# q and k arrive in 32x32 blocks and are turned by VectorE's stream transpose, from the third batch on

## The chip, the core and the metric

The kernel runs on one core of one Trainium2 chip. A core has five engines that work side by side, each with its own queue of instructions and joined by semaphores: TensorE (PE in the profile, with its weight loads as PEld), VectorE (DVE), ScalarE (ACT), GpSimd (POOL) and SyncE (SP), which here issues all DMAs. Data lie in HBM, in SBUF (on the core, 128 partitions) and in PSUM (eight banks into which TensorE writes). The metric is the device time of one execution in microseconds, the median of several runs; lower is better.

## The reference

The program is linear attention with an exponential feature map, followed by a mixer over tokens and channels. All inputs are float32 or float64 arrays; the shapes are batch 8, heads 8, sequence 576, head size 64, features 128.

```python
def phi(x):
    proj = einsum('bhsd,df->bhsf', x, w_phi)
    proj = proj - max(abs(proj), axis=-1, keepdims=True)
    return concatenate([exp(proj), exp(-proj)], axis=-1)
q_p, k_p = phi(q), phi(k)
kv  = einsum('bhsf,bhsd->bhfd', k_p, v)
z   = sum(k_p, axis=2)
num = einsum('bhsf,bhfd->bhsd', q_p, kv)
den = einsum('bhsf,bhf->bhs', q_p, z)[..., None] + 1e-06
x = (num / den) as (batch, seq, heads * 64)              # (8, 576, 512)
xt = x.transpose(0, 2, 1)
h = xt @ U @ V                                           # U (576, 32), V (32, 576): over tokens
u = x + h.transpose(0, 2, 1)
out = u + maximum(u @ w_ch1, 0) @ w_ch2                  # 512 -> 2048 -> 512
```

The order of the tokens matters to U, V and `out` alone: attention sums over tokens, and the channel part treats each token by itself.

## The kernel before

**Tiling.** Each batch has 576 tokens: 512 "main" ones, four tiles of 128 (NT = 4, SM = 512), and 64 "tail" ones (ST = 64). The tails of two batches share a tile, and all tails together form a ninth group of 512 tokens for the channel mixer. Heads are worked on in pairs: `Pair(b, j)`, 8 batches times 4 pairs. Main tokens are numbered `(p t)`: partition p of a tile holds tokens 4p to 4p+3, one in each of the four tiles, so that a partition's rows of q, k, v and `out` lie one after the other in HBM. Since `x` lies in that order, U is loaded as `(p t)` (line 155) and V's columns are permuted on VectorE (lines 176 to 179).

**Loading a pair.** `Pair.__init__` issues one DMA of 256 KB for k and one for q into `raw` (lines 248 to 251; two buffers, so k of one pair follows k of the pair before), then two for the tails into `t_r` (line 255, one buffer). `load_v` (line 262) issues four for v.

**Turning q and k.** A matmul contracts over partitions, so the 64 head dimensions of q and k must lie on partitions. `transposes` (line 276) does this on TensorE, with the identity `ident`: one for `t_r`, and for k and for q four 128x128 blocks into one PSUM bank `pT` (line 291), each block holding two tokens' 64 dimensions on its 128 partitions. In batches 0 and 1 (`split` false) one copy on ScalarE brings `pT` to SBUF as `T` (line 300), and projections run in full float32. From batch 2 on (`SPLIT = 2`) float32 is carried as a sum of two parts, high and low, of the faster type float32r: `stack` (line 271) writes the high part with a ScalarE copy (line 273) to 64 partitions and the low part with a VectorE subtraction (line 274) to the other 64, twice for each of k and q. One matmul over 128 partitions then multiplies both parts.

**The steps of a pair.** `s_project_k0`, `s_project_k1` (k features; line 371), `s_project_q0`, `s_kv0_q1` and `s_kv1` (q features and the sums over k and v; lines 394, 404, 411), `s_out0` and `s_out1` (lines 437, 450 and `normalize`). The features take the maximum of absolute values on VectorE for k, on GpSimd across partitions for q (line 335), and exponentials on ScalarE.

**The mixers.** `Tokens` multiplies by U and V (lines 521 and 537), writes u to HBM (line 539) for the later sum, and `Mixer` turns u (line 553) and runs 16 blocks of `hidden` (line 565, 12 matmuls of 128x512 into the one bank tagged `ph`, which line 570 on ScalarE and line 571 on VectorE empty into a high and a low part) and `add` (line 584, 12 matmuls). The weights come as float64 words and are converted on the core during batches 0 and 1 (`convert`, line 130, on ScalarE, VectorE and GpSimd).

**Order.** The main loop (line 775) works in a software pipeline over pairs: `cur` makes its outputs, `nxt` is projected, and `far`, two pairs ahead, is loaded and then turned in the middle of the step (`step(far.transposes)`, line 817, or in the list `fill`, line 795). The mixer of the batch before is cut into 32 chunks, which `Pace` spreads over the steps of the next batch, so that TensorE has long matmuls between the short ones of attention. The order that is written here is a priority: the framework plans each engine's instructions by a simulated timeline when the program is built, and sets semaphores; at run time each engine works through its queue in that order. Pools keep buffers by tag: `raw` two, `t_r`, `T0` and `T1` one each, PSUM three banks `at`, one `ph`, four `o`. The weights' loads are placed behind the last load of `far` (line 780).

Of the kernel before, what the change touches and what calls it, by code (L numbers as in the profile page):

```python
# [21 lines left out]
P = 128  # L22
# [3 lines left out]
def tile_kernel(  # L26
# [46 lines left out]
    def f32(ap):  # L73
        return ap.bitcast(F32)
# [76 lines left out]
    def load_uv():  # L151
# [3 lines left out]
            out=sv[:, 0:NT], in_=U[0:SM].rearrange("(p t) r w -> p t r w", t=NT))  # L155
# [13 lines left out]
        for cs in (slice(0, SM), slice(SM, S)):  # L169
# [6 lines left out]
            if cs.stop <= SM:  # L176
                ps_ = slice(cs.start // NT, cs.stop // NT)
                v_f = v_f.rearrange("r (p t) -> r t p", t=NT)
                vm = v_all[:, 0:SM].rearrange("r (t p) -> r t p", t=NT)[:, :, ps_]
# [55 lines left out]
    SPLIT = 2  # L235

    class Pair:


        def __init__(self, b, j):  # L240
# [5 lines left out]
            for n, src in enumerate((k, q)):  # L246
                m = raw.tile([P, 2, NT // 2, 2 * D], F32, tag="raw", bufs=2, name=f"raw{nm}_{n}")
                self.loaded = nc.sync.dma_start(
                    out=m.rearrange("p h s e -> p h (s e)"),
                    in_=src[b, hs, 0:SM, :].rearrange("h (p t) d -> p h (t d)", t=NT))  # L250
                self.raw.append(m)
# [10 lines left out]
        def load_v(self):  # L262
            self.vt, self.vb = (a[self.h0 // 2 % 2] for a in (vts, vbs))
            for g in range(2):
                nc.sync.dma_start(
                    out=self.vb[:, g, :, 0:D],
                    in_=v[self.b, self.h0 + g, 0:SM, :].rearrange("(p t) d -> p t d", t=NT))
# [8 lines left out]
        def transposes(self):  # L276
# [11 lines left out]
            for n in range(2):  # L288
                pT = self.ps(f"T{n}_", True)
                for c in range(NT):  # L290
                    nc.tensor.transpose(  # L291
                        out=pT[:, c * P:(c + 1) * P], in_=self.raw[n][:, c // 2, c % 2, :],
                        identity=ident)
                if self.split:
                    m = att.tile([P, 2, SM], F32R, tag=f"T{n}", name=f"T{n}_{nm}")
                    for s in range(2):
                        self.stack(pT[s * D:(s + 1) * D, :], m[:, s, :])
                else:
                    m = att.tile([P, SM], F32, tag=f"T{n}", name=f"T{n}_{nm}")
                    nc.scalar.copy(out=m, in_=pT)  # L300
# [62 lines left out]
        def project_k_split(self, g):  # L363
# [3 lines left out]
            for s in range(2):  # L367
# [5 lines left out]
                ts_ = slice(2 * s, 2 * s + 2)  # L373
# [71 lines left out]
        def out_main(self, s, qp, x):  # L445
# [7 lines left out]
            xo = x.rearrange("p (z s) c -> p s z c", s=2)[:, s, :, self.h0 * D:(self.h0 + 2) * D]  # L453
# [88 lines left out]
    class Mixer:  # L542
# [53 lines left out]
        def finish(self):  # L596
            g = self.g
            for t in range(4):
                if g < B:
# [3 lines left out]
                        out=out[g, 0:SM, :].rearrange("(p t) e -> p t e", t=NT)[:, t, :], in_=st)  # L603
# [257 lines left out]
```

## Time and profile before

| | |
|---|---|
| median of 3 runs | 1265.16 us (1265.14 to 1265.64) |
| span of the profiled execution (first to last instruction) | 1263.3 us |
| mean granted TensorE clock | 0.995 |
| first 193 us (batches 0 and 1, conversion of the weights) | TensorE busy 176.5 us |
| 193 to about 1065 us (batches 2 to 7, each about 139.7 us) | TensorE busy nearly throughout |
| from about 1068 us | the last mixers alone |
| q, k and v loads (lines 248, 255, 265, 268) | all on SyncE's queue |

The profile's page gives busy time of each engine, the granted clock and the DMA share over the span, and the chain of work that ended last. Other views of the same trace group instructions by line and shape (busy time, mean duration, idle time before them and what ended it), list waits by who waited for whom, give busy time in chosen stretches, or list instructions in order of time. An instruction's line is that of the kernel's file. "PE L291" is a matmul of line 291 on TensorE; "SPq" is a DMA issued by SyncE. The time of an execution as measured is 1.9 us longer than the profiled span.

### The profile page before, as it was taken

To read this page: it belongs to the slowest core of one execution; us is meant where nothing else is said; L and a number is where in the kernel's file an instruction comes from. 1 tells how busy PE (TensorE), PEld (TensorE's weight loads), DVE (VectorE), ACT (ScalarE), POOL (GpSimd) and SP (SyncE) were. 2 spreads that over 40 slices of the span, in tenths; PEclk is the share of its full clock that TensorE was granted. 3 is DMA by queue.
4 is the path that set the end of the run, shared out by engine and by line. 5 is a ranking of instruction groups with operands and counts; after the bars stand their busy time and mean duration, and the time that the engine had idled before them with its cause. 6 is when DMAs were issued, how large, how long until landed. Compare 5 with 4: busy or idle time off the path is not lost.

```text
span 1263.3 us, 17913 instructions
## 1 busy us (share of the span) xinstructions
PE 1234.8 (98%) x6941; PEld 1059.5 (84%) x6941; DVE 648.0 (51%) x1441; ACT 540.0 (43%) x1151; POOL 202.2 (16%) x154
## 2 busy tenths in 40 slices
PE   8989999999999999999999999999999999999997
PEld 7778777788888888888888888888888888788886
DVE  5877787745455545545455545654545542212111
ACT  6877776444443435344434434344534441111110
POOL 3444342111110111011111111111111110000000
PEclk9999998999999999999999999999999999999999
DMA  5695000411112002211122011211121002100001
GB/s 143 203 305 173 21 27 10 133 29 29 45 54 81 19 23 68 92 29 29 45 79 62 25 37 55 80 29 29 46 83 62 17 1 88 67 1 1 34 1 34
DMA packets 90100, 75.38 MB, mean 60 GB/s; under 512 B 51488, under 2 KB 76448, under 8 KB 89888
## 3 DMA queue, kind: packets, MB, share of 16 engines
q1 hardware_dynamic: 90016, 74.24, 19.2%
q8 instruction: 55, 0.90, 0.3%
q14 instruction: 29, 0.24, 0.1%
HBM read 55.35 MB, written 18.87 MB: 59 GB/s over the span
## 4 chain that ended last, share of the span: by engine, by line
PE 87%; ACT 5%; DVE 5%; issue 2%; DMA 1%; POOL 1%; SPq 0%; DVEq 0%; POOLq 0%; ACTq 0%
PE ph L565 30%; PE o L584 29%; PE kv_ps L411 7%; PE xp L450 7%; PE T L291 2%; PE pk L371 2%; PE pp L521 1%; PE xpt L437 1%; PE pt L553 1%; PE pq L394 1%; PE kv_ps L404 1%; ACT w_ab L138 1%; ACT w_ab L137 1%; PE pq L395 1%; ACT w_ab L140 1%
## 5 line engine op out<-in xcount | busy, mean ns | idle before, releaser
L565 PE MATMUL ph<-uT_hi,w 128*128 128x512 f32 x1152 | 388.2, 396 | 2.7 <-ACT uT_hi L231 2.3
L584 PE MATMUL o<-w,h_hi 128*128 128x512 f32 x1152 | 327.7, 396 | 2.2 <-ACT h_hi L570 2.0
L565 PEld LDWEIGHTS ph<-uT_hi,w 128*128 128x128 f32 x1152 | 215.9, 188 | 46.7 <-ACT uT_hi L231 3.2
L584 PEld LDWEIGHTS o<-w,h_hi 128*128 128x128 f32 x1152 | 211.4, 188 | 45.2 <-ACT h_hi L570 3.9
L571 DVE SCALAR_TENSOR_TENSOR h_lo<-ph,h_hi 128x512 fp32r<-128x512 f32 x144 | 99.2, 689 | 261.8 <-ACT h_hi L570 261.2
L565 PE MATMUL ph<-uT_lo,w 128*128 128x512 f32 x576 | 227.3, 395 | 0.5 <-DVE uT_lo L232 0.5
L570 ACT ACTIVATE h_hi<-ph 128x512 fp32r<-128x512 f32 x144 | 86.1, 598 | 306.2 <-PE ph L565 296.5
L584 PE MATMUL o<-w,h_lo 128*128 128x512 f32 x576 | 191.0, 396 | 0.0
L335 POOL PARTITION_ALL_REDUCE qp<-qp x64 | 126.5, 1979 | 340.4 <-ACT qp L334 331.3
L450 PEld LDWEIGHTS xp<-kv,qp 128*128 128x128 f32 x1024 | 122.7, 192 | 6.4 <-ACT qp L337 2.7
L565 PEld LDWEIGHTS ph<-uT_lo,w 128*128 128x128 f32 x576 | 108.7, 189 | 22.8 <-DVE uT_lo L232 1.7
L411 PEld LDWEIGHTS kv_ps<-vb,kp 128*128 128x128 f32 x1024 | 123.9, 195 | 4.2 <-issue 2.1
L450 PE MATMUL xp<-kv,qp 128*128 128x65 f32 x1024 | 123.3, 272 | 1.6 <-ACT qp L337 1.5
L584 PEld LDWEIGHTS o<-w,h_lo 128*128 128x128 f32 x576 | 106.6, 188 | 20.5
L411 PE MATMUL kv_ps<-vb,kp 128*128 128x65 f32 x1024 | 123.6, 275 | 0.0
L274 DVE TENSOR_TENSOR T<-T,T 64x512 fp32r<-64x512 f32 x96 | 66.1, 689 | 80.2 <-ACT T L273 78.9
L273 ACT CAST T<-T 64x512 fp32r<-64x512 f32 x96 | 55.9, 582 | 100.2 <-PE pq L395 73.5
L335 POOL PARTITION_ALL_REDUCE qp_t<-qp_t x32 | 25.3, 791 | 374.1 <-ACT qp_t L334 373.7
L325 ACT ACTIVATE kp<-kp 128x512 f32<-128x512 f32 x64 | 40.5, 632 | 63.0 <-DVE kp L322 48.7
L374 ACT COPY kp<-pk 128x256 f32<-128x256 f32 x96 | 35.4, 372 | 67.2 <-PE pk L371 67.0
L146 POOL INT64_ADD w_ab<-w_ab x32 | 44.4, 1387 | 88.1 <-DVE w_ab L142 49.6
L375 DVE TENSOR_TENSOR kp<-pk,kp 128x256 f32<-128x256 f32 x96 | 39.9, 418 | 30.3 <-ACT kp L374 30.0
(126 smaller groups left out, 1383.7 us busy)
## 6 DMA issues: line engine op xcount, KB each, us to landing
words<-in_moe_w_ch_dram SPq DMA_DIRECT2D x32, 512.0 KB, 7.6
raw<-in_k_dram SPq DMA_DIRECT2D x32, 256.0 KB, 2.9
raw<-in_q_dram SPq DMA_DIRECT2D x32, 256.0 KB, 3.0
vb<-in_v_dram SPq DMA_DIRECT2D x64, 128.0 KB, 2.6
u_dram<-x SPq DMA_DIRECT2D x32, 256.0 KB, 2.5
st<-u_dram SPq DMA_DIRECT2D x16, 512.0 KB, 4.3
out_dram<-st SPq DMA_DIRECT2D x32, 256.0 KB, 2.6
t_r<-in_k_dram SPq DMA_DIRECT2D x32, 32.0 KB, 2.2
```

What stands on the lines that cost most here:

```text
L146: nc.gpsimd.int64_add(a64, a64, b64)
L273: nc.scalar.copy(out=dst[0:D], in_=src)
L274: nc.vector.tensor_sub(dst[D:2 * D], src, f32(dst[0:D]))
L325: nc.scalar.activation(out=kp[:, :, 0:F], in_=kp[:, :, F:2 * F], func=AF.Exp)
L335: nc.gpsimd.partition_all_reduce(qp[:, 0, :], qp[:, 1, :], P, ReduceOp.absmax)
L375: nc.vector.tensor_tensor(out=k_w[:, ts_, :], in0=pk[:, :, 0, :], in1=kp[:, ts_, 0:F], op=ALU.add)
L411: nc.tensor.matmul(self.kv_v[:, f, g, :], kp[:, t, f * F:(f + 1) * F], self.vb[:, g, t, :], start=False, stop=(t == NT - 1), skip_group_ch ...
L450: nc.tensor.matmul(xv[:, c, :], qp[:, f, c * P:(c + 1) * P], self.kv[:, f, c // 2, :], start=(f == 0), stop=(f == 1))
L565: nc.tensor.matmul(ph, w1_part(f, l, c), r[:, c, :], start=(n == 0), stop=(n == 3 * NCC - 1))
L570: on_act = nc.scalar.activation(out=h_hi, in_=ph, func=AF.Relu)
L571: on_dve = nc.vector.scalar_tensor_tensor(out=h_lo, in0=ph, scalar=0.0, in1=f32(h_hi), op0=ALU.max, op1=ALU.subtract)
L584: nc.tensor.matmul(self.o[t], l[:, cs], w2_t[f][:, r, :], start=(f == 0 and n == 0), stop=(f == NFC - 1 and n == 2))
```

## The change

Three things change together.

1. **q and k of batches 2 to 7.** The pair's main tokens of k and of q are each loaded by eight DMAs of 32 KB instead of one of 256 KB. Each brings, for one head, one half of the 512 rows and one half of the 64 dimensions: 32 partitions, each with eight pieces of 32 float32 values (128 bytes), placed so that the tile consists of 32x32 blocks that only have to be turned in place. `nc.vector.transpose` turns all blocks of a 128x512 tile in one instruction, in SBUF. The eight TensorE transposes of the pair (four for k, four for q) and their PSUM banks are gone. The split in two parts (two ScalarE copies, two VectorE subtractions for each tensor) now reads SBUF.
2. **Token numbers.** Main tokens are numbered `(t p)`: tile t holds rows 128t to 128t+127. U is loaded so, V needs no permutation any more, `out` is written in 128 consecutive rows, and v of batches 2 to 7 is loaded as `(t p)`. The blocks of k's features (`ts_`) and of `x` (`xo`) move accordingly.
3. **Batches 0 and 1** keep their TensorE transposes. k and v stay in the old order there (only their sum over tokens counts), while q is loaded by four DMAs, each for one head and two of the four tiles, in pieces of 256 bytes.

```diff
-            out=sv[:, 0:NT], in_=U[0:SM].rearrange("(p t) r w -> p t r w", t=NT))
+            out=sv[:, 0:NT], in_=U[0:SM].rearrange("(t p) r w -> p t r w", t=NT))
...
-            if cs.stop <= SM:
-                ps_ = slice(cs.start // NT, cs.stop // NT)
-                v_f = v_f.rearrange("r (p t) -> r t p", t=NT)
-                vm = v_all[:, 0:SM].rearrange("r (t p) -> r t p", t=NT)[:, :, ps_]
...
-    SPLIT = 2
+    SPLIT, Q = 2, 32
...
-                m = raw.tile([P, 2, NT // 2, 2 * D], F32, tag="raw", bufs=2, name=f"raw{nm}_{n}")
-                self.loaded = nc.sync.dma_start(
-                    out=m.rearrange("p h s e -> p h (s e)"),
-                    in_=src[b, hs, 0:SM, :].rearrange("h (p t) d -> p h (t d)", t=NT))
+                m = raw.tile([P, 2, SM // 2], F32, tag="raw", bufs=2, name=f"raw{nm}_{n}")
+                if self.split:
+                    for i in range(4):
+                        rs = slice(i // 2 * (SM // 2), (i // 2 + 1) * (SM // 2))
+                        cs = slice(i % 2 * Q, (i % 2 + 1) * Q)
+                        for g in range(2):
+                            self.loaded = nc.sync.dma_start(
+                                out=m[i * Q:(i + 1) * Q, g, :].rearrange(
+                                    "c (j r) -> c j r", r=Q),
+                                in_=src[b, self.h0 + g, rs, cs].rearrange(
+                                    "(j c) r -> c j r", c=Q))
+                elif n == 0:
+                    self.loaded = nc.sync.dma_start(
+                        out=m, in_=src[b, hs, 0:SM, :].rearrange("h (p t) d -> p h (t d)", t=NT))
+                else:
+                    for g in range(2):
+                        for z in range(2):
+                            self.loaded = nc.sync.dma_start(
+                                out=m[:, g, z * P:(z + 1) * P].rearrange(
+                                    "p (s d) -> p s d", s=2),
+                                in_=src[b, self.h0 + g, 0:SM, :].rearrange(
+                                    "(s z p) d -> z p s d", s=2, z=2)[z])
...
+                order = "(t p) d -> p t d" if self.split else "(p t) d -> p t d"
...
-                    in_=v[self.b, self.h0 + g, 0:SM, :].rearrange("(p t) d -> p t d", t=NT))
+                    in_=v[self.b, self.h0 + g, 0:SM, :].rearrange(order, t=NT))
...
-                pT = self.ps(f"T{n}_", True)
-                for c in range(NT):
-                    nc.tensor.transpose(
-                        out=pT[:, c * P:(c + 1) * P], in_=self.raw[n][:, c // 2, c % 2, :],
-                        identity=ident)
                 if self.split:
                     m = att.tile([P, 2, SM], F32R, tag=f"T{n}", name=f"T{n}_{nm}")
+                    x_ = self.raw[n].rearrange("p h e -> p (h e)")
+                    nc.vector.transpose(out=x_, in_=x_)
                     for s in range(2):
-                        self.stack(pT[s * D:(s + 1) * D, :], m[:, s, :])
+                        here, there = (slice(i * D, (i + 1) * D) for i in (s, 1 - s))
+                        nc.scalar.copy(out=m[here, s, :], in_=x_[here])
+                        nc.vector.tensor_sub(m[there, s, :], x_[here], f32(m[here, s, :]))
                 else:
+                    pT = self.ps(f"T{n}_", True)
+                    for c in range(NT):
+                        nc.tensor.transpose(
+                            out=pT[:, c * P:(c + 1) * P],
+                            in_=self.raw[n][:, c // 2, c % 2 * P:(c % 2 + 1) * P],
+                            identity=ident)
...
-                ts_ = slice(2 * s, 2 * s + 2)
+                ts_ = slice(s, NT, 2)
...
-            xo = x.rearrange("p (z s) c -> p s z c", s=2)[:, s, :, self.h0 * D:(self.h0 + 2) * D]
+            xo = x.rearrange("p (s z) c -> p s z c", s=2)[:, s, :, self.h0 * D:(self.h0 + 2) * D]
...
-                        out=out[g, 0:SM, :].rearrange("(p t) e -> p t e", t=NT)[:, t, :], in_=st)
+                        out=out[g, t * P:(t + 1) * P, :], in_=st)
```

## The prediction

> **What bounds the kernel now.** I read the page first (engine shares), then busy time by stretches of the span, then TensorE's waits, then the timelines of TensorE, VectorE and SyncE through one batch. The page:
>
> ```profile
> PE 1234.8 (98%) x6941; PEld 1059.5 (84%) x6941; DVE 648.0 (51%) x1441; ACT 540.0 (43%) x1151; POOL 202.2 (16%) x154
> ```
>
> A busy TensorE (PE) can still be a PE that waits inside a share, so I look by stage. These are three stretches of the table by stretches: the first 64 us, the rest of batches 0 and 1, and one batch of the steady part (start:end, length, then busy us of each engine with its instruction count).
>
> ```profile
> 0.00:64.00 64.00, 57.80 (x381) 47.29 (x382) 46.60 (x123) 46.34 (x105) 27.18 (x38) 1.00 0.58 171
> 64.00:193.00 129.00, 118.72 (x680) 98.62 (x678) 101.95 (x204) 96.07 (x189) 54.31 (x39) 1.00 0.40 129
> 473.70:613.40 139.70, 139.03 (x816) 121.44 (x815) 74.33 (x171) 59.90 (x133) 18.64 (x12) 1.00 0.17 50
> ```
>
> In the steady batch PE is busy 139.03 of 139.70 us at granted clock 1.00, VectorE (DVE) 53%, ScalarE (ACT) 43%. In the first 193 us PE idles 6.2 + 10.3 = 16.5 us, while DVE and ACT are busy about three quarters of the time and the DMA engines 40 to 58%. So there are two stages with different limits: batches 0 and 1, where several things bind, and everything after, which is PE work end to end. All waits of the PE row from 334 to 1031 us (five batches; who waited, for whom, total, times, longest):
>
> ```profile
> PE ph L565 <- ACT uT_hi L231: 0.9, 2, 0.4
> PE ph L565 <- DVE uT_lo L232: 0.5, 2, 0.2
> ```
>
> 1.4 us in 697: there, a microsecond taken from PE is a microsecond off the end, as long as nothing new makes PE wait.
>
> **What the change removes: TensorE transposes.** From batch 2 on there are 6 x 4 = 24 head pairs, each with 8 transposes (4 of k, 4 of q). Matmuls overlap, so the price is not the duration of one but the distance between starts (start, us, operation, count):
>
> ```profile
> 544.58 1.03 PE L291 MATMUL T<-ident,raw 128*128 128x128 f32 x8
> 545.37 2.07 PE L584 MATMUL o<-w,h_hi 128*128 128x512 f32 x8
> 547.28 0.39 PE L565 MATMUL ph<-uT_hi,w 128*128 128x512 f32 x1
> 547.50 0.39 PE L565 MATMUL ph<-uT_lo,w 128*128 128x512 f32 x1
> ```
>
> Eight transposes take 545.37 - 544.58 = 0.79 us. The eight matmuls behind them take 1.91 us, where eight at the spacing of the undisturbed ones (547.50 - 547.28 = 0.22) take 1.76 to 1.82, the times being rounded to 0.01: the group costs another 0.09 to 0.15 us behind it. So a pair costs 0.79 (where small matmuls stand behind it anyway) to 0.94 us. I take 0.85: 24 x 0.85 = **20.4 us**, bounds 24 x 0.79 = 19.0 and 24 x 0.94 = 22.6.
>
> **What it adds on VectorE and ScalarE.** Two stream transposes of 128x512 a pair, which the trace does not show. The nearest rows are 128x512 operations from SBUF to SBUF (busy us, mean ns):
>
> ```profile
> L336 DVE TENSOR_TENSOR qp<-qp 128x512 f32<-128x512 f32 x64 | 47.5, 742 | 11.0 <-POOL qp L335 10.4
> L224 DVE TENSOR_TENSOR w<-w_ab,w 128x512 fp32r<-128x512 f32 x32 | 27.7, 877 | 3.6 <-ACT w L223 3.4
> L223 DVE CAST w<-w_ab 128x512 fp32r<-128x512 f32 x16 | 8.3, 519 | 3.4 <-POOL w_ab L146 3.4
> L180 DVE CAST v_all<-v_ab 128x512 fp32r<-128x512 f32 x1 | 1.1, 1120 | 0.0
> L182 DVE TENSOR_TENSOR v_all<-v_ab,v_all 32x512 fp32r<-32x512 f32 x1 | 1.1, 1096 | 0.0
> L274 DVE TENSOR_TENSOR T<-T,T 64x512 fp32r<-64x512 f32 x96 | 66.1, 689 | 80.2 <-ACT T L273 78.9
> ```
>
> Between 0.52 (a plain cast) and 1.12 us (a cast that reads with a stride); I take 0.74, the one in place over f32 (L336). The four subtractions a pair (L274) read SBUF alone instead of PSUM: 0.74 to 0.88 for 0.69, so at most +0.19 each. Together 2 x 0.74 + 4 x 0.19 = 2.2 us of DVE a pair, 9 a batch: 74 + 9 = 83 of some 136 us. That is far from a bound; it lies beside PE work and costs nothing itself. The ACT copies stay four a pair. What it can cost is place in the queue: DVE runs in order, and each of the two operations can stand in front of a split of `ph` (line 571), for which the one `ph` bank and so the next `hidden` wait. By the PE waits above, five batches lost 1.4 us to ACT and DVE; I allow 1 us for all six, bounds 0 and 3.
>
> **What it adds on SyncE and the DMA engines.** A split pair now issues 16 loads of 32 KB instead of 2 of 256 KB, in pieces of 128 bytes: 2 tensors x 2 heads x 512 rows x 2 halves = 4096 pieces. The costs of an issue (min/median/max ns of the issuing instruction), and landing times:
>
> ```profile
> L255 SPq DMA_DIRECT2D t_r<-in_k_dram x32: 615/627/747, 1.7 to 961.7; - x32
> ...
> raw<-in_k_dram SPq DMA_DIRECT2D x32, 256.0 KB, 2.9
> ...
> t_r<-in_k_dram SPq DMA_DIRECT2D x32, 32.0 KB, 2.2
> ```
>
> A t_r load has the new ones' 32 KB and an access of three dimensions, so I take its 0.62 us: 16 x 0.62 = 9.9 us of SP a pair, 5.0 for one tensor, and 2.2 to 2.9 to land: 12.8 us for both. Whether the engines keep up: in the window 509 to 515 us only two vb and two vt loads run, 1216 packets of 256 bytes; in 545 to 549 us nearly all is raw in packets of 1 KB.
>
> ```profile
> q1 hardware_dynamic: 1216, 0.30, 21.9%
> ...
> DMA packets 823, 0.60 MB, mean 149 GB/s; under 512 B 319, under 2 KB 822, under 8 KB 822
> q1 hardware_dynamic: 822, 0.58, 50.4%
> ```
>
> The first gives 0.219 x 16 x 6 us / 1216 = 17.3 ns a packet; the second, less 319 such, (32.3 - 5.5) us / 503 = 53 ns for 1 KB. A packet of 128 bytes should lie under 17.3 and cannot well exceed 53: 4096 / 16 = 256 on each engine, 4.4 us a pair, at most 13.6. I take 17.3; the SP queue is then the slower side. The Trainium skill ("DMA: Bandwidth & Descriptors", Rules for kernel authors) says against this change that transfers under 64 KB are mostly overhead, and (Anatomy of one DMA, for GpSimd's queue) fits about 2.0 us of fixed cost to each DMA; summed one behind the other, 16 of them would be an estimated 32 us a pair in place of the 12.8. The trace agrees with the fixed part (t_r lands in 2.2), and whether it is summed is the last rival.
>
> Is there room for 12.8 us? These are SP, DVE and PE rows around one pair:
>
> ```profile
> 545.22 0.55 SPq L248 DMA_DIRECT2D raw<-in_k_dram  x1
> 545.86 0.42 SPq L248 DMA_DIRECT2D raw<-in_q_dram  x1
> ...
> 547.46 0.69 DVE L274 TENSOR_TENSOR T<-T,T 64x512 fp32r<-64x512 f32 x1 [0.32 <-ACT T L273]
> 550.83 0.69 DVE L571 SCALAR_TENSOR_TENSOR h_lo<-ph,h_hi 128x512 fp32r<-128x512 f32 x1 [2.67 <-ACT h_hi L570]
> ...
> 556.00 0.69 DVE L274 TENSOR_TENSOR T<-T,T 64x512 fp32r<-64x512 f32 x1
> ...
> 559.98 0.40 PE L371 MATMUL pk<-w_hl,T 128*128 128x256 f32 x2
> ```
>
> Before, a raw buffer came free with PE's last transpose (545.37). Now it is held until the last split of the turned data: for k 548.2, for q 556.7 (q's second split waits until the previous pair's last use of T1 is over, as it does now). From 556.7, q's eight loads are issued by 561.7 and landed by 564.6. A batch of 139.7 us has four pairs, so the next transposes come some 35 us after 544.58, near 579.5, and the first projection from them another 15 later (for this pair 544.58 against 559.98). 15 us to spare; the other things behind the 14 added issues on SP (8.7 us: the pair's t_r and v loads, u_dram, st and out) have use times of the same order. So the loads cost nothing here, and would cost if a plan puts the turn close behind the landing (first rival).
>
> **Batches 0 and 1** keep their PE transposes, but q now comes in 4 loads of 256-byte pieces instead of 1, ahead of t_r, weights and v on the same queue.
>
> ```profile
> 2.54 0.61 SPq L255 DMA_DIRECT2D t_r<-in_q_dram  x1
> ...
> 4.94 0.45 PE L282 MATMUL tT<-ident,t_r 128*128 128x128 f32 x1 [0.98 <-DMA t_r<-in_q_dram]
> ```
>
> 4 x 0.62 less the one issue of 0.42 (545.86) is +2.1 us of SP in each of 8 pairs. The start hangs on this queue: PE's first real work waits for t_r, behind q. That moves by up to 2.1. Two more places can pay: pair 1, whose loads stand behind pair 0's, and a wait of the chain for v behind weights (start, us):
>
> ```profile
> 70.68 8.58 DMA vb<-in_v_dram
> ```
>
> Bounds 0 (the plan issues t_r first, later slack absorbs) and 6 (all three in full); I take 3.3. Against it, V's copy loses its stride: L180 and L182, 1120 and 1096 ns on DVE in a stretch where DVE is full, should fall towards L223's 519 and L224's 877, -0.8. Net **+2.5**. U's one load has four times as many pieces (512 of 256 bytes, 0.5 us on 16 engines at 17.3 ns); v in rows of 128, `kp` written in every second block and `out` in consecutive rows keep their counts and sizes; I cost all of these at nothing: they lie beside PE work.
>
> **Sum.** Profiled span 1263.3 us; the median of the runs is 1265.16, 1.9 more, which I carry over. 1263.3 - 20.4 + 1.0 + 2.5 = 1246.4 span, **1248** as measured. Own range: best 1265.2 - 22.6 - 0.8 = 1242; worst 1265.2 - 19.0 + 3 + 6 = 1255.
>
> **Rivals.**
> *DVE stands in front of a late load (slower).* The planner orders each engine's queue when the program is built, from its own timing. DVE is idle nearly half the time, so the plan may put a stream transpose right where it believes the load lands. If it believes raw's old landing of 2.9 us while the last piece comes 12.8 after the first issue, DVE stands still for 9.9 us, and the split of `ph` with it. The idle time ahead of h_lo (2.67 at 550.83) covers part; the rest, 7.2 us, reaches PE once a pair: 24 x 7.2 = 173, about 1421 us; with half the error 24 x 2.3 = 55, about 1303. It decides from (1265.2 - 1248) / 24 = 0.7 us of PE idle a pair. For it: the load's shape is new. Against: the plan has been close on DMA so far, as the only wait of a computing engine for a DMA from 334 to 1031 us is
>
> ```profile
> DVE xt L807 <- DMA u_dram<-xt: 0.9, 2, 0.4
> ```
>
> Chance 0.11 of slower; 0.05 that it takes part of the gain (1255 to 1262).
> *The gain is handed back.* DVE's two added operations a pair, 1.5 us, stand ahead of the split of `ph` at a moment without idle time in front, and half of that reaches PE: 24 x 0.75 = 18, so 1248 + 18 = 1266. Against: 0.3 us of waits a batch now. 0.05.
> *The loads serialise.* If 16 loads go one behind the other at t_r's 2.2 us, a pair's loads take 35.2 us; with 2 x 0.74 for the turn and 2.8 until the buffer is free (545.37 to 548.2), 39.5 a pair against 139.7 / 4 - 0.85 = 34.1: 24 x 5.4 = 130, about 1378 us. Against: two issues 0.64 us apart (545.22 and 545.86) overlap already, each landing in 2.9. 0.02.
>
> **How the numbers follow.** The forecast has 0.77. Its own range, 1242 to 1255, with the partial loss up to 1260 makes 8 in 10: 1242 to 1260. 0.2% is 2.5 us, about what a measurement here can tell. Faster by more: 0.77 + 0.05 = 0.82; within: 0.05; slower: 0.11 + 0.02 = 0.13.
>
> **What would show it.** L291 falls from 256 to 64 matmuls; a steady batch shrinks from 139.7 to about 136.4 us with PE still full; the DVE transposes read 0.5 to 1.1 us each; raw's loads take some 10 us of SP a pair and end over 10 us ahead of use; the first PE transposes of t_r start near 6 to 7 us instead of 4.94. I am wrong if DVE shows waits on raw of over 2 us in most pairs, if PE idles over 0.5 us a pair in steady batches, or if the first 193 us grow by more than 6.

## The result, and the profile after

The changed kernel takes 1259.2 us (median of 7 runs, 1253.6 to 1263.0) against 1265.6 us of before beside it (1265.1 to 1269.3): ratio 0.9933, 95% interval 0.9903 to 0.9962. That is about 8 us faster, where 17 were forecast: the right side and inside the range of 1242 to 1260, but less than half the size.

The page of the changed kernel, engine shares:

```profile
PE 1221.9 (97%) x6749; PEld 1044.6 (83%) x6749; DVE 680.5 (54%) x1489; ACT 541.6 (43%) x1151; POOL 204.0 (16%) x154
```

TensorE is busy 12.9 us less, but the span is only 7.1 us shorter (1256.2 against 1263.3). So TensorE is idle for longer: 34.3 us against 28.5. The table by stretches, for the first 64 us, the rest of batches 0 and 1, and one steady batch (from the first transposes of one mixer to those of the next), shows that "busy" is no fixed measure either; the third number from the right is the granted clock:

```profile
0.00:64.00 64.00, 56.17 (x343) 46.51 (x344) 39.51 (x107) 43.10 (x98) 25.39 (x36) 0.95 0.58 166
64.00:193.00 129.00, 119.79 (x702) 100.83 (x700) 101.79 (x213) 94.50 (x187) 53.49 (x39) 0.99 0.41 127
512.79:649.71 136.92, 136.37 (x783) 118.27 (x781) 79.25 (x178) 60.38 (x132) 18.73 (x12) 1.00 0.21 50
```

The steady batch went from 139.70 to 136.92 us with TensorE as full as before and 33 matmuls fewer in the record (32 transposes are gone). That is 2.8 us a batch, 0.70 us a pair. The first 64 us, however, hold 38 matmuls fewer than before, at a clock of 0.95.

What the turn became, groups by line (busy us, mean ns, then idle time just before and what ended it):

```profile
L311 DVE TENSOR_TENSOR T<-raw,T 64x512 fp32r<-64x512 f32 x96 | 70.8, 737 | 29.3 <-ACT T L310 27.0
...
L307 DVE STREAM_TRANSPOSE raw<-raw 128x512 f32<-128x512 f32 x48 | 34.1, 711 | 56.6 <-DMA raw<-in_q_dram 34.8 <-DMA raw<-in_k_dram 14.6 <-DMA t_r<-in_k_dram 2.5
L315 PE MATMUL T<-ident,raw 128*128 128x128 f32 x64 | 10.0, 291 | 0.0
```

A stream transpose of 128x512 takes 711 ns (0.74 was taken), a subtraction 737 (0.74 to 0.88). But VectorE stood 49.4 us in front of raw loads. Whether that costs anything is read one engine further on: the waits of the PE row from 334 to 1031 us, all of them:

```profile
PE pk L391 <- DVE uT_lo L228: 1.3, 5, 0.3
PE ph L585 <- ACT uT_hi L227: 0.3, 2, 0.2
```

1.6 us, as before (1.4). VectorE waits there in time that it has to spare.

**Three terms.** Each profiled span can be split into TensorE's idle time (span less busy), what the clock took (span times one less the mean granted clock), and the rest, TensorE's work at full clock. It is a rough split, since the clock has three digits (0.6 us), but it shows where the gain went. Before: 28.5 idle, 1263.3 x 0.005 = 6.3 to the clock, 1228.5 of work. After: 34.3 idle, 1256.2 x 0.009 = 11.3 to the clock, 1210.6 of work. The work fell by 17.9; idle time gave back 5.8 and the clock 5.0. These are single executions. The median run of the changed kernel had a clock of 0.988, so the typical run lost some 4 us more to it than the profiled one; so did the kernel before, whose median clock was 0.992 in 55 runs beside the experiments. Means over the runs stand further down.

**Where the idle time and the clock are lost.** The start of the changed kernel, SyncE and TensorE rows in order of time:

```profile
1.23 1.99 SPq L260 DMA_DIRECT2D raw<-in_q_dram  x4
3.26 0.74 SPq L269 DMA_DIRECT2D t_r<-in_k_dram  x1
4.05 0.61 SPq L269 DMA_DIRECT2D t_r<-in_q_dram  x1
...
6.26 0.45 PE L297 MATMUL tT<-ident,t_r 128*128 128x128 f32 x1 [2.30 <-DMA t_r<-in_q_dram]
```

q's four issues take 1.99 us (0.50 each), t_r is issued 1.5 us later and the first turn comes at 6.26 us in place of 4.94. The four issues stand in each pair of the first two batches, and the load of U, issued at 16.75 before, is issued at 22.11. From there a chain can be followed over ScalarE and VectorE to TensorE:

```profile
22.11 0.59 SPq L154 DMA_DIRECT2D u_st<-in_moe_U_dram  x1
...
25.74 0.38 ACT L137 ACTIVATE u_ab<-u_st 128x160 uint16<-128x160 uint16 x1 [1.29 <-DMA u_st<-in_moe_U_dram]
...
28.34 0.52 DVE L164 CAST u_all<-u_ab 128x128 fp32r<-128x128 f32 x3 [0.15 <-POOL u_ab L146]
...
31.52 0.42 DVE L449 TENSOR_TENSOR x<-xp,den 128x256 f32<-128x256 f32 x1
...
32.00 0.71 PE L424 MATMUL kv_ps<-vt,kp_t 128*128 128x130 f32 x4 [2.43 <-DVE x L449]
```

The same three places in the kernel before:

```profile
16.75 0.58 SPq L154 DMA_DIRECT2D u_st<-in_moe_U_dram  x1
...
20.95 0.39 ACT L137 ACTIVATE u_ab<-u_st 128x160 uint16<-128x160 uint16 x1 [1.06 <-DMA u_st<-in_moe_U_dram]
...
26.56 1.19 PE L291 MATMUL T<-ident,raw 128*128 128x128 f32 x8 [1.02 <-DVE x L429]
```

ScalarE waited for U before, too (1.06 us, now 1.29), but U's conversion now comes 4.8 us later in the run. It sits on VectorE just where the normalised outputs of a pair are wanted, and TensorE waits 2.43 us for those, where it waited 1.02. Then, in stretches of 2 us, the clock (third number from the right):

```profile
32.00:34.00 2.00, 2.00 (x18) 2.00 (x18) 1.31 (x3) 1.80 (x6) 1.07 (x1) 1.00 0.30 70
34.00:36.00 2.00, 2.00 (x13) 1.91 (x12) 0.19 (x1) 1.44 (x3) 0.48 (x1) 0.57 0.94 312
36.00:38.00 2.00, 2.00 (x11) 2.00 (x11) 1.97 (x6) 0.92 (x3) 1.66 (x2) 0.50 1.02 365
38.00:40.00 2.00, 2.00 (x9) 1.81 (x9) 0.90 (x2) 0.00 (x0) 1.00 (x2) 0.50 1.07 384
40.00:42.00 2.00, 2.00 (x6) 1.15 (x6) 0.72 (x2) 0.00 (x0) 0.00 (x0) 0.72 0.51 116
42.00:44.00 2.00, 2.00 (x20) 1.98 (x18) 1.85 (x6) 1.19 (x3) 0.86 (x1) 1.00 0.03 8
```

Two microseconds after the wait the clock halves, for some 6.8 us, while TensorE is completely busy: (0.43 + 0.50 + 0.50 + 0.28) x 2 = 3.4 us are lost. If the drop is put down to the wait, the 2.4 us have cost 5.8. Three other kernels with the same order of matmuls up to there show a wait of 2.45 us at the same place, and their clock falls there as well.

### The profile page after: what moved, and what is told of

Same layout as the page of the kernel before. It is cut to its first block, busy times and chain, and to the rows that moved or that the text cites. A ratio compares the mean times of both kernels' runs of the same rounds, so it can differ in the third digit from the quotient of the medians.

```text
span 1256.2 us, 18188 instructions
## 1 busy us (share of the span) xinstructions
PE 1221.9 (97%) x6749; PEld 1044.6 (83%) x6749; DVE 680.5 (54%) x1489; ACT 541.6 (43%) x1151; POOL 204.0 (16%) x154
## 4 chain that ended last, share of the span: by engine, by line
PE 84%; DVE 9%; ACT 4%; issue 1%; SPq 1%; DMA 1%; POOL 1%; DVEq 0%; ACTq 0%; POOLq 0%
PE ph L585 30%; PE o L604 28%; PE kv_ps L431 8%; PE xp L470 7%; PE pk L391 2%; PE pp L541 1%; DVE w L220 1%; PE kv_ps L424 1%; PE pq L414 1%; DVE uT_lo L228 1%; PE pt L573 1%; PE pq L415 1%; ACT w_ab L137 1%; ACT w_ab L138 1%; PE xpt L457 1%
## 5 line engine op out<-in xcount | busy, mean ns | idle before, releaser
L604 PE MATMUL o<-w,h_lo 128*128 128x512 f32 x576 | 198.0, 396 | 0.0
L311 DVE TENSOR_TENSOR T<-raw,T 64x512 fp32r<-64x512 f32 x96 | 70.8, 737 | 29.3 <-ACT T L310 27.0
L310 ACT CAST T<-raw 64x512 fp32r<-64x512 f32 x96 | 59.3, 618 | 29.2 <-PE pq L415 24.9
L357 ACT ACTIVATE qp<-qp 128x512 f32<-128x512 f32 x64 | 40.5, 632 | 66.2 <-DVE qp L356 65.8
L307 DVE STREAM_TRANSPOSE raw<-raw 128x512 f32<-128x512 f32 x48 | 34.1, 711 | 56.6 <-DMA raw<-in_q_dram 34.8
```

Source lines behind the costliest of these rows:

```text
L310: nc.scalar.copy(out=m[here, s, :], in_=x_[here])
L311: nc.vector.tensor_sub(m[there, s, :], x_[here], f32(m[here, s, :]))
L357: nc.scalar.activation(out=qp[:, 0, :], in_=qp[:, 1, :], func=AF.Exp)
L604: nc.tensor.matmul(self.o[t], l[:, cs], w2_t[f][:, r, :], start=(f == 0 and n == 0), stop=(f == NFC - 1 and n == 2))
```

## The experiments

Theory A: the forecast's main term holds, and what is missing was lost in batches 0 and 1, because q's four issues on SyncE delay everything queued behind them, and the idle time that this makes on TensorE then brings the clock down as well. Theory B: the turn on VectorE, or its small loads, is what gives the gain back. For each experiment the ratio to the kernel before that ran beside it is the measure, since that kernel's own median moved from 1265.6 to 1267.4 us between the sessions; the three terms are of the one profiled execution of each.

| kernel | median us | ratio to before (95%) | idle | to the clock | work |
|---|---|---|---|---|---|
| before | 1265.6 | 1 | 28.5 | 6.3 | 1228.5 |
| after | 1259.2 | 0.9933 (0.9903 to 0.9962) | 34.3 | 11.3 | 1210.6 |
| TensorE turns, rest of the change kept | 1275.9 | 1.0067 (1.0045 to 1.0089) | 32.7 | 14.0 | 1227.0 |
| one load of q | 1250.6 | 0.9869 (0.9846 to 0.9893) | 29.0 | 8.7 | 1210.7 |
| two loads of q | 1264.1 | 0.9969 (0.9951 to 0.9986) | 35.6 | 12.6 | 1210.6 |
| wide loads for the stream transpose | 1259.4 | 0.9945 (0.9923 to 0.9967) | 32.9 | 15.1 | 1209.1 |
| q's four loads from ScalarE | 1257.0 | 0.9916 (0.9902 to 0.9931) | 28.6 | 15.1 | 1211.4 |
| q's four loads behind t_r | 1252.4 | 0.9894 (0.9881 to 0.9907) | 30.1 | 11.3 | 1208.9 |
| q in four loads of long pieces | 1255.0 | 0.9910 (0.9897 to 0.9923) | 33.5 | 11.3 | 1210.3 |
| three filling matmuls for one | 1256.8 | 0.9925 (0.9913 to 0.9938) | 27.1 | 3.8 | 1223.5 |
| each turn done three times | 1263.5 | 0.9964 (0.9940 to 0.9987) | 36.4 | 19.0 | 1210.7 |
| behind t_r, two filling matmuls | 1258.1 | 0.9932 (0.9903 to 0.9961) | 30.4 | 12.6 | 1218.3 |
| from ScalarE, two filling matmuls | 1251.3 | 0.9871 (0.9836 to 0.9907) | 28.7 | 5.0 | 1216.2 |
| before, q's load behind t_r | 1265.5 | 0.9998 (0.9971 to 1.0025) | 27.5 | 8.8 | 1226.8 |

**TensorE turns again.** The loads in short pieces of batches 2 to 7 are replaced by q's four-load form for both tensors, and the transposes go back to TensorE; the numbering and the loads of batches 0 and 1 stay as changed.

```diff
...
-                elif n == 0:
+                if n == 0 and not self.split:
...
+                pT = self.ps(f"T{n}_", True)
+                for c in range(NT):
+                    nc.tensor.transpose(
+                        out=pT[:, c * P:(c + 1) * P],
+                        in_=self.raw[n][:, c // 2, c % 2 * P:(c % 2 + 1) * P],
+                        identity=ident)
...
-                    nc.vector.transpose(out=x_, in_=x_)
...
+                        self.stack(pT[s * D:(s + 1) * D, :], m[:, s, :])
...
```

> The new token numbers and the four loads of q, now for k too, in all batches, but every turn on TensorE as before the change. So only the stream transposes and their 128-byte loads are taken back. Theory A (the change takes 14 to 15 us of PE work away at full clock, and the early part, with q's loads and idle stretches that lower PE's clock, gives about 8 back): slower than the kernel before by 3 to 10 us, 1268 to 1275, with a mean clock below the 0.995 of before, and in the steady batches 139.7 us as before. Theory B (the loss is VectorE standing in front of late 128-byte loads, in all batches): like before, 1264 to 1267, since nothing waits for such loads here.

Measured 1275.9 us, ratio 1.0067, just above the range of Theory A. This splits the result in two. The turn alone, from this kernel to the changed one, is worth 1.0067 - 0.9933 = 1.34%, 17 us (12 to 22 by the two intervals); the rest of the change costs 0.67%, 8.5 us (5.7 to 11.3). The forecast had 20.4 - 1.0 = 19.4 and 2.5 for the two. Here the work is 1227.0, nearly as before: what is lost is all idle time and clock.

**One load of q.** q of batches 0 and 1 goes back to one load in the old order.

```diff
-                elif n == 0:
+                else:
                     self.loaded = nc.sync.dma_start(
                         out=m, in_=src[b, hs, 0:SM, :].rearrange("h (p t) d -> p h (t d)", t=NT))
-                else:
-                    for g in range(2):
-                        for z in range(2):
...
```

> The changed kernel, but in batches 0 and 1 q comes in one load of 256 KB as before the change, so that its tokens there stand in the old order, which this kernel does not put right; all else is the changed kernel. Theory A: the first turn starts near 4.9 us again, the clock drops between 30 and 100 us go, mean clock 0.993 or more, 1250 to 1254 us. Theory B: no change, 1257 to 1261.

1250.6 us, ratio 0.9869: 0.64% less than the changed kernel, 8.1 us (some 5 us to either side by the intervals). That is the whole price of the early part as far as can be measured. What is left, 1.31% or 16.6 us less than the kernel before, is what the turn alone gives, and so the numbering of U, V and `out` costs nothing that can be seen. Its early stretches, to be set beside those above:

```profile
0.00:64.00 64.00, 57.98 (x380) 47.52 (x381) 45.56 (x120) 46.25 (x105) 27.23 (x38) 1.00 0.64 191
64.00:193.00 129.00, 124.02 (x697) 104.92 (x697) 101.37 (x210) 95.15 (x188) 53.91 (x39) 0.96 0.38 118
```

380 matmuls in the first 64 us, as before (381), at full clock; the changed kernel had done 343. The drops of the clock up to 100 us did not all go, as Theory A had it: the stretch from 80 to 96 us reads 0.68.

**Two loads of q.**

```diff
                     for g in range(2):
-                        for z in range(2):
...
+                        self.loaded = nc.sync.dma_start(
+                            out=m[:, g, :].rearrange("p (t d) -> p t d", t=NT),
+                            in_=src[b, self.h0 + g, 0:SM, :].rearrange("(t p) d -> p t d", t=NT))
...
+            order = "p (s z) c -> p s z c" if self.split else "p (z s) c -> p s z c"
+            xo = x.rearrange(order, s=2)[:, s, :, self.h0 * D:(self.h0 + 2) * D]
```

> The changed kernel, but in batches 0 and 1 q comes in two loads, one per head, in the same 256-byte pieces, with the tiles of x numbered to match. Two issues less on SyncE in each of eight pairs. Theory A: between the changed kernel and the one with a single load, 1253 to 1258. Theory B: no change, 1257 to 1261.

1264.1 us: worse than four loads, a miss for Theory A in the form "so much per issue". The first turn starts at 5.78 us, between the two, but TensorE is idle for 35.6 us; 3.8 us of that lie between 48 and 64 us, and from 64 to 80 us the clock is 0.70. So the number of issues alone does not set the price; why this arrangement is the worst was not found.

**Wide loads.** The loads of 128-byte pieces are replaced by one load of 256 KB a tensor in every batch.

```diff
-                if self.split:
-                    for i in range(4):
...
-                elif n == 0:
+                if n == 0 or self.split:
                     self.loaded = nc.sync.dma_start(
```

> The changed kernel with the stream transposes, but from batch 2 on k and q come in one load of 256 KB each, in rows of 1 KB as before the change, so that the turned blocks do not hold what they should; the arithmetic is otherwise left as it is. Theory A: VectorE's waits for raw shrink, but PE is not held by them in the steady batches (0.6 us a batch), so at most 2 us are won outside clock drops: 1255 to 1260. Theory B: the waits of 57 us in front of the stream transposes fall below 15 and 6 us or more are won: 1248 to 1253.

1259.4 us, ratio 0.9945 against 0.9933, the intervals overlap. The change's most striking feature, 384 loads of 128-byte pieces in place of 48 large ones, is free here as far as can be measured, and a steady batch takes 136.9 to 137.0 us with either, but for one of 138.6 in the changed kernel in which the clock fell. VectorE's waits in front of raw did not shrink but grew (35.7 and 31.9 us for q and k, against 34.8 and 14.6): the plan puts the turn right behind the landing, whatever the load. Theory B falls for the loads.

**Where q's issues stand, and what they carry.** Three kernels tell issue time from piece size and place.

```diff
-                            self.loaded = nc.sync.dma_start(
+                            nc.scalar.dma_start(
```

> Theory A (the early price of some 8 us is SyncE's issue time: q's four loads stand in front of t_r, v, U and V, and what arrives late lets TensorE and then its clock fall): with q's four loads of batches 0 and 1 issued by ScalarE, SyncE has its old queue, U's load is issued near 16.8 us again, and the time falls to 1249 to 1254; ScalarE pays some 2 us a pair where it has slack. Theory B (the 256-byte pieces of q cost, whoever issues them): 1257 to 1261.

```diff
-                else:
-                    for g in range(2):
-                        for z in range(2):
-                            self.loaded = nc.sync.dma_start(
...
             self.t_r = raw.tile([P, 2 * D], F32, tag="t_r", bufs=1, name=f"t_r{nm}")
...
+            if not self.split:
+                m = self.raw[1]
+                for g in range(2):
+                    for z in range(2):
+                        self.loaded = nc.sync.dma_start(
...
```

> The same four loads of q on SyncE, issued behind t_r instead of in front of it. Theory A in its narrow form (the first turn of t_r, 1.3 us late, is what costs): back to 1250 to 1254. Theory A in its wide form (v, U and V behind the pairs' loads are late too, and they still are): 1255 to 1260, with the first turn near 4.9 us. Theory B: 1257 to 1261.

```diff
+                            ps_ = slice(z * D, (z + 1) * D)
+                            rs = slice(z * (SM // 2), (z + 1) * (SM // 2))
...
-                                out=m[:, g, z * P:(z + 1) * P].rearrange(
-                                    "p (s d) -> p s d", s=2),
-                                in_=src[b, self.h0 + g, 0:SM, :].rearrange(
-                                    "(s z p) d -> z p s d", s=2, z=2)[z])
+                                out=m[ps_, g, :],
+                                in_=src[b, self.h0 + g, rs, :].rearrange(
+                                    "(p t) d -> p (t d)", t=NT))
```

> q of batches 0 and 1 in four loads, but of 1024-byte pieces and in the old order of tokens (its rows come out in another order there, which this kernel doesn't put right). Theory A (number of issues): as the changed kernel, 1257 to 1261. Theory B (size of the pieces, or the order of the tokens): as with one load, 1249 to 1253.

Four loads of long pieces leave TensorE as idle as four of short ones (33.5 against 34.3, and 29.0 with one load), and their first turn is as late (6.74 us). So the size of the pieces is not the cause of the idle time. Its time, 1255.0, lies between the two expectations; the profiled execution is within 1.1 us of the changed kernel's (1255.1 against 1256.2, both at a clock of 0.991), and the intervals of the two ratios overlap. Issued behind t_r the first turn starts at 4.51, idle time falls to 30.1, and the time to 1252.4 (ratio 0.9894), although U is still issued at 22.27 us: the place of t_r is the larger part, so the narrow form of Theory A. Issued by ScalarE they leave TensorE as idle as before the change (28.6), with the first turn at 5.26 and U issued at 20.36; yet 1257.0 came out, a time of Theory B's range and not of Theory A's. The clock takes 15.1 us: against the kernel with one load (29.0 and 8.7) it is the whole difference. So the idle time goes with the issues on SyncE, and the clock's loss here does not.

**The clock itself.** `keep_busy` runs filling matmuls on zeros at steps that have no mixer work; it does three in place of one here.

```diff
-                    keep_busy(1, True)
+                    keep_busy(3, True)
...
-                keep_busy(1, True)
+                keep_busy(3, True)
```

> The changed kernel with three filling matmuls in place of one at each step where the mixer has nothing to give. If the early price is paid through TensorE's clock, which falls after stretches with idle time, the clock stays up and the time falls to 1250 to 1256 at a mean clock of 0.993 or more. If the price is the idle time itself, the filling changes nothing or adds up to 10 us: 1259 to 1270.

Between the two expectations, and the table says why. The clock now reads 1.00 where it had fallen (start of the stretch, TensorE busy, clock; the changed kernel had 13.52 and 1.00, then 16.00 at 0.79):

```profile
16.00:32.00 16.00, 15.87 (x108) 12.52 (x107) 10.57 (x37) 9.90 (x23) 4.40 (x6) 1.00 0.48 123
32.00:48.00 16.00, 15.65 (x111) 13.03 (x111) 12.64 (x32) 10.49 (x27) 6.84 (x7) 1.00 0.59 177
```

Against the changed kernel the clock gives back 7.5 us and idle time 7.2, and the filling, 62 more matmuls, is 12.9 us of work: 1.8 us remain. So most of the early drops do follow TensorE's gaps, since filling the gaps takes them away (the mean clock is 0.994 to 0.998 in five runs), but the filling costs almost what it gains.

**VectorE's dose.** Each turn is done three times in place.

```diff
-                    nc.vector.transpose(out=x_, in_=x_)
+                    for _ in range(3):
+                        nc.vector.transpose(out=x_, in_=x_)
```

> Each stream transpose is done three times in place (three turns give what one gives), so VectorE gets another 4 x 0.71 us a pair. The question is why a pair gave 0.70 us and not 0.85. Theory S (the transposes' own spacing and their neighbours on TensorE; VectorE's work lies beside it): the time stays within 4 us of the changed kernel, a steady batch stays at 136.9 to 137.3 us. Theory D (VectorE's queue hands back 0.15 us a pair for its 1.42 us of turning): another 0.30 us a pair, 24 x 0.30 = 7 us at least, and a steady batch of 138.1 us or more.

68 us more of VectorE (101.7 for 34.1) cost 0.31%, 4 us. Four steady batches of the profiled execution, the slowest of twelve:

```profile
382.74:519.65 136.91, 136.29 (x783) 118.23 (x781) 89.40 (x194) 61.32 (x132) 19.39 (x12) 1.00 0.22 51
519.65:656.86 137.21, 136.57 (x782) 118.33 (x781) 89.91 (x194) 60.99 (x132) 19.38 (x12) 1.00 0.22 51
656.86:797.14 140.28, 138.19 (x783) 119.52 (x781) 89.62 (x193) 61.24 (x132) 19.03 (x12) 0.99 0.21 49
797.14:934.97 137.83, 136.57 (x783) 118.25 (x781) 90.54 (x195) 61.13 (x132) 19.04 (x12) 1.00 0.22 51
```

Two of them are as short as with one turn; in the other two TensorE waits for an operation of VectorE on x (2.2 us in all), and the clock reads 0.99 in one of them. Theory S holds for the single turn: VectorE hands back nothing that can be seen in the steady part. With three times the dose the edge is near: two of the four batches lie above its 137.3.

**Two combinations.** Each of the two better orders with two filling matmuls in place of one (the edits are those above).

> q's four loads behind t_r, and two filling matmuls in place of one at the early steps. If the loss left in that order is mostly the clock (0.990 against 0.997 with three filling ones), and a second filling matmul costs about half of what two cost: the clock reads 0.994 to 0.997 and the time 1247 to 1252. If the filling costs as much as the clock gives back, as with three: 1252 to 1257.

> q's four loads from ScalarE's queue, and two filling matmuls in place of one. At full clock this order is worth as much as one load of q (span times clock 1239.6 against 1240.1); if the clock is all that it lacks: 1248 to 1252 at 0.994 or more. If filling costs what it gives: 1255 to 1258.

The first is a miss: 1258.1, worse than without filling (1252.4). The clock is not the reason: over all runs of the two kernels the clock takes 8.9 us with the filling and 12.2 without, but idle time and work together are 9.1 us more, where the same filling costs 5.4 in the other order. Why it costs more here was not found. The second does what it was meant to: 1251.3 us, ratio 0.9871, 0.62% less than the changed kernel, with the new numbering in full. It loses 5.0 us to the clock and 28.7 to idle time, about as the kernel before (6.3 and 28.5), and pays 4.8 us of work for the filling. It beats both kernels.

**A control.** In the kernel before, q's one load of batches 0 and 1 is issued behind t_r.

> The kernel before, with one thing moved: in batches 0 and 1 q's one load is issued behind t_r and not in front of it. No count or size changes. Theory A (SyncE's issue time is the price): the first turn starts 0.5 us earlier, and the time is that of before or less, 1262 to 1267. Theory C (any edit of the first batches gives another plan for them, and plans differ by several microseconds through idle time and clock): more than 3 us away from before, to either side, with a mean clock that differs by 0.003 or more.

1265.5 us, ratio 0.9998: nothing, although the first turn starts at 4.34 in place of 4.94. So not every edit of the first batches moves the time, and Theory C, as a general rule, falls. It also says that a 0.6 us earlier first turn is worth nothing by itself in the old plan.

## Why the prediction was right and wrong

**What bounds it** was right: a steady batch is TensorE end to end before and after, and TensorE's waits there stayed at 1.6 us.

**The transposes** were taken at 0.85 us a pair, with bounds of 0.79 and 0.94. Measured: 0.70 in the steady batch (2.8 / 4), (1227.0 - 1210.6) / 24 = 0.68 by the work of the kernel with TensorE's turns, 17 / 24 = 0.71 by its time (of these 17 us some 4 are a difference in the clock, by the table below). The mechanism was right; by the steady batch the term is 16.8 us in place of 20.4, and by every measure below the lower bound of 19.0. The eight starts do go (0.77 us a pair over four batches), but the cost added for the group behind them did not come back, and the transpose of t_r, which used to run into them, now has 0.07 us before the next start in place of 0.03 (16 of them over four batches: 1.08 us for 0.45).

**VectorE and ScalarE** were right in price (711 ns for 740) and in being beside the path: the allowed 1 us was not needed, and three times the dose cost 4 us. **The first rival** is half right, and the half is worth learning: the plan does put the turn right behind the landing, and VectorE stands in front of raw for 49 us in all. It costs nothing, by these rows because the splits of `ph` behind it have slack, and because the turned q is used only some 15 us later (turned at 552.54, first projection at 567.70):

```profile
552.54 0.71 DVE L307 STREAM_TRANSPOSE raw<-raw 128x512 f32<-128x512 f32 x1 [1.78 <-DMA raw<-in_q_dram]
554.02 0.69 DVE L591 SCALAR_TENSOR_TENSOR h_lo<-ph,h_hi 128x512 fp32r<-128x512 f32 x1 [0.77 <-ACT h_hi L590]
```

So the sign set for it, over 2 us of waits for raw in most pairs, was a bad one: in 334 to 1031 us they come to some 2.1 us a pair (32.3 for q and 9.9 for k in 20 pairs), and TensorE still waits for 1.6 us in all. The sign had to be TensorE's wait. **Serialised loads** were wrong: eight issues follow each other at under 0.5 us (0.62 was taken) and each lands in 1.9. The Trainium skill ("DMA: Bandwidth & Descriptors", Rules for kernel authors) has transfers under 64 KB as mostly overhead; the traces show that this overhead overlaps between loads: eight are issued in 3.8 us and each lands 1.9 us after its issue, and wide loads gave 0.9945 against 0.9933.

**Batches 0 and 1** are the step that failed. "Net +2.5", with bounds of 0 and 6 for q's loads, was SyncE's issue time and the places where it could pay. Measured is +8: 8.5 by the kernel with TensorE's turns, 8.1 by the kernel with one load of q. The issue time was near (0.50 us each, 0.62 taken) and so was the first turn, at "6 to 7 us" (6.26). What failed is the pricing of these loads as a delay alone. The sum had no term for the granted clock, although the trace of before has it at 0.90 from 193 to 225 us. And a late load also moves what VectorE has in front of TensorE: with U's conversion 4.8 us later, TensorE's wait behind it is 2.4 us in place of 1.0. V's copies, taken at -0.8, fell by 0.5 us on VectorE (3.0 to 2.5). With TensorE's turns the shortfall of the median times can be divided: of 8.4 us, 2.4 are in the turn (19.4 forecast, 17 measured) and 6.0 here (2.5 forecast, 8.5 measured).

Going back to one load of q frees 5.3 us of idle time and 2.6 of the clock in the profiled executions. But the clock differs between runs of one kernel (0.986 to 0.992 in seven runs of the changed one), and the span and the clock of every run are known. So the split can be made over all runs: what the clock took, and span times clock, which is idle time and work together (means, us).

| kernel | runs | idle time and work | to the clock |
|---|---|---|---|
| before | 55 | 1255.4 | 10.2 |
| after | 7 | 1242.6 | 14.4 |
| TensorE turns, rest of the change kept | 6 | 1255.8 | 18.5 |
| one load of q | 6 | 1240.2 | 9.0 |
| two loads of q | 12 | 1246.0 | 15.9 |
| q in four loads of long pieces | 4 | 1242.4 | 11.0 |
| q's four loads from ScalarE | 6 | 1239.5 | 14.6 |
| q's four loads behind t_r | 4 | 1239.1 | 12.2 |

One load of q frees 2.4 us of the first kind and 5.4 of the clock; the kernel with TensorE's turns differs from before by 0.4 and 8.3. So the larger part of the price is the clock, for which the sum had nothing, and the delay itself is no more than about what was taken for it (3.3 us). The delay goes with the issues in front of t_r: four long pieces keep it, ScalarE's queue and the place behind t_r take it away, and only the kernel with two loads does not fit. The clock's part does not go with the issues, since q from ScalarE still loses 14.6 us; what decides between a loss of 9 and one of 15 us stays open. Every one of these kernels is also planned anew (with one load of q the order of TensorE's matmuls parts from the changed kernel's at the 61st), and these runs do not separate what the new plan alone does. The two columns are also not quite independent: among the runs of one kernel, those that lose 1 us more to the clock show some 0.3 us less of the rest.

## What to carry to other kernels

Where one engine is the bound, price an edit in the stage where that engine is full and, separately, in the stage where it is not: here the same change gave 17 us in the one and lost 8 in the other, through loads that had nothing to do with its purpose. In a stage with gaps, count a queue's issue time as delay for everything behind it, and give the clock a term of its own, since it can take more than the delay. Loads that the next step waits for belong ahead of others in the queue where the others are many: here that was worth 0.4% with four loads of q, and nothing with one. A wait of an off-path engine is no sign of a cost until the engine that sets the end waits for it too.

## What the runs showed of the hardware

The granted clock can halve after a short gap: a single wait of 2.43 us was followed, some 2 us later, by some 6.8 us at 0.50 with TensorE full. With the wait at the same place in the three kernels named below the clock was lower still (0.68, 0.59 and 0.68 from 32 to 48 us, for 0.79). But such a gap is neither enough nor needed. In the kernel before, and in the same kernel with q's load behind t_r, the transposes that start near 77.7 us wait 1.90 us for the same copy on ScalarE; this is the stretch behind the wait, first in the kernel before, then in the other (the clock is the third number from the right):

```profile
78.00:80.00 2.00, 1.75 (x16) 1.53 (x14) 1.48 (x2) 1.95 (x6) 2.00 (x2) 1.00 0.59 110
...
78.00:80.00 2.00, 2.00 (x11) 2.00 (x10) 1.52 (x2) 1.92 (x6) 2.00 (x2) 0.50 0.47 92
```

And at 672.6 us of the changed kernel the clock halves (0.52 to 676.1 us) where no wait of TensorE from 640 to 680 us is over 0.3 us. The clock of the first ten microseconds is not to be relied on: eight transposes of the changed kernel take 1.92 us at 6.50 and 1.04 us at 14.49, and both stretches read 1.00.

In stretches of 16 us the clock reads 0.89, 0.79 or 0.68, that is 1.8, 3.4 or 5.1 us lost, steps of about 1.7, which is half of 3.4. The Trainium skill ("TensorE: Matmul & The Clock Gate", Part 1: The HAM clock gate) describes half rate after an idle window of about 3.4 us; the step agrees, but here the clock halved behind waits of 2.4 and 1.9 us, and once where none was over 0.3.

The same order of work meets this in different numbers. The changed kernel and the ones with TensorE's turns, with wide loads and with three turns run the same first 500 matmuls in the same order (one record is missing in one trace), yet the 500th starts at 89.2 us in the first and at 94.6 to 94.9 us in the other three: the three have more drops of the clock up to there, and each is 5.5 to 5.7 us behind. Differences of a few microseconds between two such executions are the clock's.

A stream transpose of 128x512 float32 in place takes 711 ns, as long as an elementwise operation of two inputs of the same size (742), and loads in 128-byte pieces cost no more here than loads in rows of 1 KB (0.9933 against 0.9945).
